# Output stores of 64 rows cut into two by rows, in a fused attention and GEGLU kernel

## The chip, the cores and the metric

The kernel runs on one core of a Trainium2 chip. A core has TensorE (matmul; PE in the profile, and PEld for its weight loads), VectorE (DVE), ScalarE (ACT), GpSimd (POOL) and SyncE (SP), each with its own stream of instructions that it works through in order, and 16 DMA engines that all of them share. The metric is the time of one launch on the device, in microseconds. Engines wait for each other, and for DMAs, on semaphores.

## The reference

Attention without softmax (scores are scaled, cut at zero, squared and divided by the length), then a GEGLU feed-forward block on the joined heads:

```python
scores = scale * np.matmul(q, k.transpose(0, 1, 3, 2))      # q, k, v: 8 x 12 x 448 x 64
attn = np.maximum(scores, 0.0) ** 2 / S
attn_out = np.matmul(attn, v)
x = attn_out.transpose(0, 2, 1, 3).reshape(B * S, H * D)    # 3584 x 768
g = x @ w_gate                                              # 768 x 1536
gelu = 0.5 * g * (1.0 + erf(g / sqrt(2)))
out = (gelu * (x @ w_val)) @ w_out                          # 3584 x 768, float32
```

## The kernel before

The eight batches go through four stages that overlap: loading q, k and v (GpSimd issues the loads, which turn float32 into bfloat16 on the way); transposing q and k per third of a batch's heads (by TensorE for the first two batches, afterwards by a regrouping copy on VectorE, `qkr`, L475, and two DMA transposes that SyncE issues, L480); scores, relu (ScalarE, L714), square (VectorE, L728) and the product with v; then the feed-forward block. TensorE works on quarters of its array (64 x 64), and matmuls for one half of the rows run beside those for the other. The products with the weights use seven multiplications for a 2 x 2 block of sub-matrices in place of eight, so sums and differences of operands are made on VectorE (`s`, `ts`, `ws`, `wt`).

The last product makes 28 tiles of 128 tokens by 768 columns. A tile consists of two chunks of 64 tokens, and lies in SBUF as `osb` (pool with four buffers). Its two column halves are opened by copies on ScalarE (L1225) and finished by additions on VectorE (L1223). A chunk's 64 rows lie in 64 partitions; in the output, row p of chunk c of a batch is row 7 p + c, so a store writes 64 rows of 3072 bytes that are 7 rows apart. `emit_store` (L1238) issues one chunk. Tiles are made in groups `gr` of two (t = 2 gr and 2 gr + 1), 14 groups in all. For the first twelve groups a tile's two chunks are stored whole by SyncE as soon as its two last additions are done (48 stores of 192 KB); for the last two groups (LAST = 2) the column halves are stored apart, chunk 0 by SyncE and chunk 1 by ScalarE (16 stores of 96 KB).

A planner (`run_plan`) places all instructions of all engines in an order once, when the program is built, from costs written in the code; the order then is fixed. An `osb` tile takes a buffer when its first copy is placed, and this copy waits in the program for all stores of the tile that had the buffer four tiles before. Scores go to one pair of PSUM banks (`sp`), so that the scores of the next unit wait for the relu of the last one.

SyncE's queue holds the DMA transposes and the stores in one order. A transpose may be held back until a given matmul has run, and waits for the transpose before it. All DMAs that SyncE and ScalarE issue take one of eight completion semaphores in turn, and an issue waits, where it isn't clear from the order anyway, for the DMA eight before it.

Of the kernel before, what the change touches and what calls it, by code (L numbers as in the profile page):

```python
# [276 lines left out]
def kernel(  # L277
# [10 lines left out]
    nc = tc.nc  # L288
# [6 lines left out]
    P = 64  # L295
# [5 lines left out]
    d_model, d_ff = moe_w_gate.shape  # L301
# [56 lines left out]
    HALF = (slice(0, P), slice(P, 2 * P))  # L358
# [744 lines left out]
                "7": lambda: wt_op[3, i]}[name]()  # L1103

    LAST, HELD = 2, 8
    sums, osb, stored = {}, {}, {}
    CUTS = 0, KH - 1, KH

# [51 lines left out]
    def add_product(at, gr, name, final):  # L1160
# [27 lines left out]
        else:  # L1188
            t, half = source
            have = [[st["made_by"](b, half * KH + f) for b in sorted({b for b, _ in chunks[t]})] for f in range(KH)]  # L1190

        def emit(r, fc):
# [4 lines left out]
            for j in range(2):  # L1197
# [13 lines left out]
                for fc in range(KH)] for r in range(2)]  # L1211
        st["last", name] = ops[1][-1]
        left, right = slice(0, OGS), slice(OGS, 2 * OGS)
        t, cols, added = {"1": (t0, left, False), "2": (t0, left, True), "3": (t0, right, False),
                          "6": (t1, left, False), "4": (t1, left, True),
                          "7": (t1, right, False), "5": (t1, right, True)}[name]
# [11 lines left out]
        engine = "DVE" if added else "ACT"  # L1228
# [9 lines left out]
        def emit_store(j, engine=nc.sync, part=slice(0, d_model)):  # L1238
            b, c = chunks[t % 2][j]
            rows = out[b * S:(b + 1) * S, :].rearrange("(p c) d -> c p d", c=SC)  # L1240
            return engine.dma_start(rows[c, :, part], osb[t][HALF[j], part])  # L1241

        def held_store(*args):
            def emit():
                ins = emit_store(*args)
                if op.mark is not None:
                    tc.add_manual_dep(ins.ins, op.mark.ins.name, SYNC, reason="pace")

            op = Op("SP", 0.6, emit, [rd] if len(args) > 1 else st["done", t], lag=0.0 if len(args) > 1 else 2.5, prio=-1)
            op.hold = gr >= HELD  # L1250
            return op

        if name in "2345":
            st["done", t] = [*st.get(("done", t), ()), rd]
            if gr >= B * SC // 4 - LAST:
                SP.append(held_store(0, nc.sync, cols))
                ACT.append(Op("ACT", 0.45, lambda: emit_store(1, nc.scalar, cols), [rd], prio=-1))
            elif len(st["done", t]) == 2:
                stored[t] = [held_store(j) for j in range(2)]
                SP.extend(stored[t])  # L1260
# [66 lines left out]
    for at, item in placed:  # L1327
# [4 lines left out]
        else:  # L1332
            _, gr, name = item
# [71 lines left out]
    for kind, lo, hi in pairs:  # L1405
        if kind == "with":
            upper.append((tau[place[lo]], hi))
        else:
# [8 lines left out]
            t = tau[min(behind + 1, len(PE0))]  # L1417
# [79 lines left out]
```

## Time and profile before

| what | value |
|---|---|
| time, median of 2 runs | 401.8 us (401.79 to 401.81) |
| span of the profiled execution, first to last instruction | 394.9 us |
| time less span: what lies around the program | 6.9 us (the profile gives no time of its own for its execution beside the span) |
| TensorE busy | 386.3 us, 98% |
| VectorE, ScalarE, GpSimd busy | 78%, 66%, 25% |
| DMA, mean | 114 GB/s, 85567 packets |
| mean granted TensorE clock | 0.998 |

In the lines below, an instruction's group is told as line, engine, operation and `out<-in` with the tile's names. "SPq" and "ACTq" are the sequencers of these engines, which wait and issue DMAs. In a timeline the columns are start, duration and what ran, with the idle time before it and what ended that in brackets. For a line or tile in a window, three numbers behind a count are the shortest, median and longest duration in ns, then the first and last start in us; "DMA to landing" is the time from a DMA's issue to its last completion. A row that begins with two times (a:b) is a stretch: its length, then for PE, PEld, DVE, ACT and POOL the busy time and the number of instructions, the granted TensorE clock, the DMA engines' mean busy share, and GB/s. A row of a DMA queue has packets, MB, and the time of its packets as a share of 16 engines' time in that stretch, which can go over 100% when packets overlap.

### The profile page before, as it was taken

How to read it: one execution, taken by the hardware profiler on the slowest of the kernel's cores; microseconds unless marked ns; L12 is line 12 of the kernel's file. 1: busy time of each engine (PE TensorE's matmuls, PEld its weight loads, DVE VectorE, ACT ScalarE, POOL GpSimd, SP SyncE). 2: the span in 40 equal slices, each digit the busy share in tenths (PEclk: the TensorE clock that was granted, in tenths of full speed). 3: DMA queues.
4: the chain of work that ended last, by engine and by line, in shares of the span. 5: the costliest groups of instructions: out<-in, count | busy, mean ns of one | idle time of the engine just before them, and what ended most of it. 6: DMA issues, size and time to landing. Idle time of an engine off the chain costs nothing.

```text
span 394.9 us, 22904 instructions
## 1 busy us (share of the span) xinstructions
PE 386.3 (98%) x10570; PEld 358.4 (91%) x10573; DVE 309.6 (78%) x522; ACT 258.7 (66%) x401; POOL 97.2 (25%) x156
## 2 busy tenths in 40 slices
PE   7999999999999999999999999999999999999995
PEld 3458889999999999999999999989999999999994
DVE  3885779968797499999797779758988999866772
ACT  5866872357677767787786478765787886535541
POOL 7656523322233323232332123310211000000000
PEclk9999999999999999999999999999999999999999
DMA  8999999988999969887999598880763501121134
GB/s 110 186 199 199 197 209 185 112 103 83 161 148 175 152 85 143 93 132 121 113 148 108 124 122 111 139 83 11 103 105 56 125 6 43 45 45 45 43 85 120
DMA packets 85567, 45.12 MB, mean 114 GB/s; under 512 B 46048, under 2 KB 82400, under 8 KB 85472
## 3 DMA queue, kind: packets, MB, share of 16 engines
q0 software_dynamic: 46944, 24.39, 49.9%
q1 hardware_dynamic: 37888, 18.49, 26.4%
q8 instruction: 82, 1.34, 1.4%
q10 hardware_dynamic: 640, 0.79, 0.6%
q14 instruction: 13, 0.11, 0.1%
HBM read 48.76 MB, written 11.01 MB: 151 GB/s over the span
## 4 chain that ended last, share of the span: by engine, by line
PE 93%; DVE 2%; DMA 2%; POOL 1%; issue 1%; ACT 0%; ACTq 0%; POOLq 0%
PE ff L365 85%; PE sp L365 7%; DMA qk<-in_k_dram 2%; DVE attnT L728 1%; PE sp L646 1%; POOL qk L424 1%; DVE xT L792 0%; PE ff L646 0%; ACTq L1241 0%; ACT osb L1225 0%; ACT rl L714 0%; PE ff L567 0%; DVE osb L1223 0%; DVE qkT L650 0%; POOL ident masks.py:199 0%
## 5 line engine op out<-in xcount | busy, mean ns | idle before, releaser
L714 ACT ACTIVATE rl<-sp 128x896 bf16<-128x896 f32 x168 | 152.1, 919 | 50.4 <-PE sp L365 45.1
L365 PE MATMUL ff<-xT,wg 64*64 64x224 bf16 (+1 forms) x2304 | 183.7, 299 | 0.6 <-issue 0.6
L365 PEld LDWEIGHTS <-wv 64*64 64x64 bf16 x2304 | 127.7, 107 | 4.4
L365 PEld LDWEIGHTS <-wg 64*64 64x64 bf16 x2304 | 123.3, 107 | 5.0 <-issue 0.5
L365 PE MATMUL ff<-xT,wv 64*64 64x448 bf16 x1056 | 120.8, 349 | 0.0
L728 DVE TENSOR_TENSOR attnT<-rl 128x1792 bf16<-128x1792 bf16 (+1 forms) x98 | 92.2, 952 | 6.6 <-ACT rl L714 6.2
L365 PEld LDWEIGHTS <-ws 64*64 64x64 bf16 x1872 | 92.3, 107 | 1.4 <-issue 1.0
L365 PEld LDWEIGHTS <-s 64*64 64x64 bf16 x1344 | 81.6, 107 | 1.8
L365 PE MATMUL ff<-attnT,v 64*64 64x448 bf16 (+1 forms) x768 | 79.7, 326 | 0.7 <-DVE attnT L728 0.6
L365 PE MATMUL ff<-ts,wv 64*64 64x224 bf16 x1248 | 78.7, 256 | 0.0
L365 PE MATMUL ff<-ts,ws 64*64 64x224 bf16 x1248 | 77.6, 256 | 0.0
L365 PE MATMUL sp<-qkT 64*64 64x448 bf16 (+1 forms) x768 | 74.6, 328 | 0.7 <-issue 0.3
L365 PE MATMUL ff<-wo,s 64*64 64x384 bf16 x672 | 63.4, 323 | 0.0
L966 DVE TENSOR_TENSOR part<-ff,part 128x448 f32<-128x448 f32 x78 | 47.5, 622 | 20.1 <-PE ff L365 16.4
L365 PEld LDWEIGHTS <-uT 64*64 64x64 bf16 x1008 | 62.5, 107 | 0.7
L365 PE MATMUL ff<-wt,s 64*64 64x384 bf16 x672 | 61.4, 322 | 0.0
L365 PE MATMUL ff<-wo,uT 64*64 64x384 bf16 x672 | 60.7, 322 | 0.0
L962 ACT COPY part<-ff 128x448 f32<-128x448 f32 x78 | 41.3, 534 | 12.4 <-PE ff L365 11.2
L443 POOL DMA_DIRECT2D v<-in_v_dram x48 | 29.6, 620 | 80.3 <-ACT rl L714 44.3
L365 PEld LDWEIGHTS <-v 64*64 64x64 bf16 x768 | 44.7, 107 | 4.1 <-issue 1.7
L424 POOL DMA_DIRECT2D qk<-in_q_dram x43 | 27.6, 642 | 80.0 <-ACT rl L714 59.5
L1049 DVE TENSOR_TENSOR uT<-gel,ff 128x448 bf16<-128x448 bf16 x44 | 27.3, 620 | 22.4 <-PE ff L365 11.0
(51 smaller groups left out, 423.9 us busy)
## 6 DMA issues: line engine op xcount, KB each, us to landing
out_dram<-osb SPq DMA_DIRECT2D x48, 192.0 KB, 3.3
v<-in_v_dram POOLq DMA_DIRECT2D x48, 128.0 KB, 4.1
wg<-in_moe_w_gate_dram POOLq DMA_DIRECT2D x6, 384.0 KB, 10.4
wv<-in_moe_w_val_dram POOLq DMA_DIRECT2D x6, 384.0 KB, 11.0
wo<-in_moe_w_out_dram POOLq DMA_DIRECT2D x4, 576.0 KB, 14.9
qk<-in_q_dram POOLq DMA_DIRECT2D x18, 128.0 KB, 3.5
qk<-in_k_dram POOLq DMA_DIRECT2D x18, 128.0 KB, 4.3
qk<-in_q_dram POOLq DMA_DIRECT2D x18, 96.0 KB, 3.8
```

Of the source, the lines that this page charges most:

```text
L365: ins = nc.tensor.matmul(o, lhsT, rhs, start=start, stop=stop, skip_group_check=onto, tile_position=(P * row, P * col))
L424: return nc.gpsimd.dma_start(qk16[b, m][HALF[i], r0:r0 + h1 - h0, cols], src[b, h0:h1].rearrange("h (p c) d -> p h (c d)", c=SC)[:, :, cols])
L443: return nc.gpsimd.dma_start(v16[b, m][HALF[i], h0 % 4:h0 % 4 + h1 - h0, :, :], v[b, h0:h1].rearrange("h (p c) d -> p h c d", c=SC)[:, :, ...
L646: blocks.add(nc.tensor.transpose(t[HALF[j], c, :], src[:, 2 * r + j, c, :], ident[:, :], tile_position=(0, P * j)))
L714: relu.ins = nc.scalar.activation(duo["rl"][:, u % 2, :, :], box[0][:, :, 0:S], AF.Relu).ins
L728: nc.vector.tensor_tensor(a[:, part], duo["rl"][:, part], duo["rl"][:, part], op=ALU.mult)
L962: rd.ins = nc.scalar.copy(st["t", name][:, :], box[0][:, 0:S]).ins
L966: rd.ins = nc.vector.tensor_tensor(t[:, :], box[0][:, 0:S], t[:, :], op=ALU.add).ins
L1049: u_op[b, fc].ins = nc.vector.tensor_tensor(uT[b][:, fc, :], gel.pop((b, fc))[:, :], box[0][:, 0:S], op=ALU.mult).ins
```

## The change

A store of all 768 columns from SyncE is cut by rows into two DMAs that are issued one behind the other, in the same place of the order. The place of the cut goes through a list of eight by the store's number (4 gr + 2 (t mod 2) + j): 64 (whole), 61+3, 57+7, 49+15, 55+9, 52+12, 56+8, 60+4. Each of the eight occurs six times among the 48 stores; 42 stores are cut. The half-width stores at the end are as before. What is stored, and from where, doesn't change. A wait on a particular matmul, where there is one, is attached to the first of the two.

```diff
     LAST, HELD = 2, 8
+    CUT = 64, 61, 57, 49, 55, 52, 56, 60
     sums, osb, stored = {}, {}, {}
...
         def emit_store(j, engine=nc.sync, part=slice(0, d_model)):
             b, c = chunks[t % 2][j]
             rows = out[b * S:(b + 1) * S, :].rearrange("(p c) d -> c p d", c=SC)
-            return engine.dma_start(rows[c, :, part], osb[t][HALF[j], part])
+            first = CUT[(4 * gr + 2 * (t % 2) + j) % len(CUT)] if engine is nc.sync and part == slice(0, d_model) else P
+            ins = engine.dma_start(rows[c, 0:first, part], osb[t][j * P:j * P + first, part])
+            if first < P:
+                engine.dma_start(rows[c, first:P, part], osb[t][j * P + first:(j + 1) * P, part])
+            return ins
```

The instructions of TensorE, VectorE, ScalarE and GpSimd are the same ones in the same order; SyncE's queue has 42 DMAs more, and the turn of the eight semaphores shifts accordingly. ScalarE's copy that takes over a buffer then waits for three or four DMAs of the former tile in place of two.

## The prediction

> **What bounds the kernel now.** I read the profiled execution's page first: span, busy shares, the chain that ended last, the DMA queues and the issues.
>
> ```profile
> span 394.9 us, 22904 instructions
> ...
> PE 386.3 (98%) x10570; PEld 358.4 (91%) x10573; DVE 309.6 (78%) x522; ACT 258.7 (66%) x401; POOL 97.2 (25%) x156
> ...
> q1 hardware_dynamic: 37888, 18.49, 26.4%
> ...
> PE 93%; DVE 2%; DMA 2%; POOL 1%; issue 1%; ACT 0%; ACTq 0%; POOLq 0%
> ...
> out_dram<-osb SPq DMA_DIRECT2D x48, 192.0 KB, 3.3
> ```
>
> TensorE is busy for 386.3 of 394.9 us and carries 93% of the last chain. So 394.9 - 386.3 = 8.6 us is all that any gain could come from, and whatever stops TensorE, which runs its instructions in a fixed order, is added whole. The 48 stores that change are not on the chain. The question is therefore what a later landing of a store holds up. Three things can wait for one: the next DMAs on the same queue, above all the transposes that feed the scores; the reuse of one of the four osb buffers, which ScalarE opens with a copy; and the end of the program. For that I went through SyncE's timeline and the copies, looking for the store whose landing has the least time behind it. It is the first one that is cut in the changed kernel, the second half of the first osb tile. SyncE around it:
>
> ```profile
> 101.39 2.08 SPq L480 DMA_TRANSPOSE qkT<-qkr  x1
> 103.53 1.22 SPq L1241 DMA_DIRECT2D out_dram<-osb  x2
> 105.96 1.25 SPq L480 DMA_TRANSPOSE qkT<-qkr  x1
> 107.26 1.22 SPq L1241 DMA_DIRECT2D out_dram<-osb  x2
> 109.21 1.26 SPq L480 DMA_TRANSPOSE qkT<-qkr  x1
> ```
>
> The pair at 103.53 is the whole store (64 rows) and the one that becomes 61+3; the pair at 107.26 becomes 57+7 and 49+15. The first pair by source line and window (the second is issued at 104.2), then ScalarE's copies into osb in a window of their own, then ScalarE's and TensorE's timelines:
>
> ```profile
> L1241 SPq DMA_DIRECT2D out_dram<-osb x2: 582/588/593, 103.5 to 104.2; - x2
> ...
> DMA to landing us min/median/max: 3.9/4.9/5.8
> ```
> ```profile
> L1225 ACTq EVENT_SEMAPHORE  x1: 1275/1275/1275, 108.8 to 108.8; - x1
> ```
> ```profile
> 110.07 0.48 ACT L1225 COPY osb<-ff 128x384 f32<-128x384 f32 x1 [0.41 <-PE ff L365]
> 110.44 0.92 ACT L714 ACTIVATE rl<-sp 128x896 bf16<-128x896 f32 x1
> ...
> 115.11 0.48 ACT L1225 COPY osb<-ff 128x384 f32<-128x384 f32 x1 [0.55 <-PE ff L365]
> ```
> ```profile
> 111.51 0.44 PE L365 MATMUL sp<-qkT 64*64 64x224 bf16 x8
> ```
>
> The second store lands at 104.2 + 5.8 = 110.0. ScalarE's sequencer stands in a wait from 108.8 for 1.275 us, until 110.0, and its copy starts at 110.07. This copy is the fifth tile's first write and in the program waits for every store of the first tile, since it takes over its buffer. The idle time is put down to a matmul, but the landing is equally late: no cover is left. Behind the copy on ScalarE stands a relu (110.44 to 111.36), which frees the one pair of PSUM banks into which the scores at 111.51 go. TensorE has 0.15 us to spare.
>
> **The change part by part.** Six stores stay whole; the 42 others become two, so SyncE issues 42 more DMAs. Its issue takes 0.59 us (row above): 25 us on an engine that mostly waits, at most 1.2 us a pair of stores. I cost that at nothing; without the cover it would be part of the landing times below. Every engine's own order is as before, and the semaphores only rotate.
>
> What matters is how the rows are dealt out. A window with two whole stores and little else, as DMA queues:
>
> ```profile
> DMA packets 161, 0.41 MB, mean 137 GB/s; under 512 B 32, under 2 KB 32, under 8 KB 160
> ...
> q1 hardware_dynamic: 160, 0.39, 60.3%
> ```
>
> 160 packets are 128 rows and 32 small ones: 64 rows and 16 small packets a store, one small packet for each DMA engine and four rows each. All DMAs on this queue have row counts that 16 divides, so how 61 rows go isn't shown. The ends: dealt as evenly as can be (at most four rows an engine, no cost), or only in equal shares, and then 61, a prime, goes to one engine, 57 to three by 19, 49 to seven by 7, and 55, 52, 56 and 60 to 11, 13, 14 and 15 by five or four. Equal shares are what the rows show wherever I look, so I take the second end.
>
> The Trainium skill, "DMA: Bandwidth & Descriptors", section "Why a DMA increments its semaphore by 16 and not by 1", says that a DMA of this kind uses the largest count up to 16 that divides the slowest dimension, and that 127 partitions go to one engine. By it the sum would be the one below; no run here shows it yet.
>
> Price of a row on one engine, from two windows that hold stores (0.97 us and 2.10 us long):
>
> ```profile
> q1 hardware_dynamic: 220, 0.40, 108.5%
> ```
> ```profile
> q1 hardware_dynamic: 152, 0.39, 86.0%
> ```
>
> 0.40 MB are 130 rows of 3072 bytes in 0.97 us on 16 engines: 0.12 us a row, for stores that had queued behind a transpose (110.08 to 111.05). 0.39 MB in 2.10 us give 0.26 us, for stores that met empty queues and may have been limited by their issue (329.8 to 331.9). 57 rows of a 61-row store queue behind others of their own, which is like the first: 0.12.
>
> The sum:
> 1. The busiest engine gets 61 rows where it had four: 57 x 0.12 = 6.8 us later, landing at 116.8. The ends: 5.5 (the engine that gets them may have been done 1.3 us before the last one, since the landing of 110.0 is that of the slowest) and 57 x 0.26 = 14.8. Loads that share this engine are in between: two are issued on GpSimd at 108.3 and 110.0, some 2 us of it at most, and the next wait for a stalled ScalarE.
>
> ```profile
> 108.31 0.99 POOL L424 DMA_DIRECT2D qk<-in_q_dram  x1 [3.84 <-ACT rl L714]
> 109.96 0.61 POOL L424 DMA_DIRECT2D qk<-in_q_dram  x1 [0.66 <-ACT rl L714]
> ```
>
> 2. ScalarE's copy, relu and TensorE's scores all move by 6.8 us: +6.8. DVE, and the transposes that come next, gain that time, so they don't add.
> 3. The copy of 115.11 needs the stores of 107.26: 19+1+7+1 = 28 rows behind the 61 on one engine, 3.4 us and a transpose of about 1 us, against 5.04 us between the two copies. Nothing, with an end of 3.
> 4. TensorE stands still for more than 6 us, and its clock falls when it does. Stretches at the end, and the warm-up at the start beside the scores:
>
> ```profile
> 390.00:390.80 0.80, 0.73 (x10) 0.30 (x5) 0.00 (x0) 0.27 (x1) 0.00 (x0) 1.00 0.79 221
> 390.80:393.00 2.20, 0.00 (x0) 0.00 (x0) 0.00 (x0) 0.48 (x1) 0.00 (x0) 1.00 0.72 191
> 393.00:394.90 1.90, 0.00 (x0) 0.00 (x0) 0.00 (x0) 0.00 (x0) 0.00 (x0) 0.55 0.13 45
> ```
> ```profile
> L365 PE MATMUL sp<-qkT 64*64 64x448 bf16 (+1 forms) x768 | 74.6, 328 | 0.7 <-issue 0.3 <-ACT qkT L617 0.2
> L1430 PE MATMUL ff<-warm 128*64 128x512 bf16 x16 | 3.3, 590 | 1.2 <-DVE table L353 1.2
> ```
>
> TensorE ends at 390.7, and the mean of 0.55 from 393.0 on is that of a clock which goes to a half at about 393.2, some 2.4 us later. The first matmuls, 590 ns for 512 columns against 328 for 448, show the slow state, for the 3.3 us that they last. Half speed for 3.3 us loses 1.7. Ends: 0 (no fall) and 3.3.
>
> The Trainium skill, "TensorE: Matmul & The Clock Gate", section "Part 1: The HAM clock gate (the "warmup" mystery)", puts the fall after an idle window of about 3.4 us and the return after a busy one. By that the term would be the same 1.7; the trace's 2.4 us is shorter, and the trace holds no stall within the work.
>
> 5. The five other stores of 61 rows (issued at 146.0, 222.0, 249.4, 310.3, 355.0). The tightest follow-ups:
>
> ```profile
> L480 SPq DMA_TRANSPOSE qkT<-qkr x1: 1222/1222/1222, 152.4 to 152.4; - x1
> DMA to landing us min/median/max: 4.6/4.6/4.6
> ```
> ```profile
> 170.24 0.35 PE L365 MATMUL sp<-qkT 64*64 64x448 bf16 x1
> ```
> ```profile
> L1225 ACT COPY osb<-ff x6: 479/480/482, 377.9 to 384.8; 128x384 f32<-128x384 f32 x6
> ```
>
> The transpose behind the store of 146.0 lands at 157.0, and the scores that read it (the fourteenth of 24 thirds, 32 matmuls each of the x768) begin at 170.24: 13.2 us of cover for 6.8. The last 61-row store, at 355.0, is wanted by the second of the copies from 377.9 on. Nothing; with rows at 0.26 us the first would be late by 1.6.
>
> Sum: 6.8 + 0 + 1.7 + 0 = 8.5. The profiled execution's span is 394.9, and the median of the runs lies 6.9 above it, which stays: 401.8 + 8.5 = 410.3, rounded to 410.5 (+2.2%). What a measurement of this kernel can tell from no change is 2%, or 8.0 us: up to 409.8.
>
> **The rivals.**
> - Short stall: 5.5 us, and the clock stays or the phase is kind: 407 to 409. For it: the landing's 5.8 us belongs to the slowest engine. Against: the loads in between.
> - Costlier rows: 0.26 us a row, or ScalarE waiting a second time (step 3) and one transpose late: 14.8 + 1.7 + 3 + 1.6 = 21, so up to 422; a part of it gives 413 to 418.
> - Not slower: the change doesn't do what I say, since 61 rows are dealt four to an engine. The landing stays near 110.0, only the 0.6 us for issuing three more rows may show: 401.8 to 402.4. It decides in favour of this as soon as the first cut store lands within 6 us of its issue. For it: every DMA in the trace uses all 16 engines.
> - Faster by 2% would need nearly all of the 8.6 us in which TensorE is idle, most of which no store touches.
>
> **How the numbers follow.** Forecast 0.48 (own range 408.5 to 413), short stall 0.22, costlier 0.17, even dealing 0.12, faster 0.01. The range 404 to 418 leaves out even dealing (0.12), faster (0.01) and the top of the costlier case (0.06). Slower: 0.17 and 0.41 of the forecast's 0.48, whose lower edge is within 2%: 0.58. Same: 0.22 + 0.12 + 0.07 = 0.41. Faster: 0.01.
>
> **What would show it.** Right: SyncE's first cut store takes 12 us or so to land, while the later ones of 55, 52, 56 and 60 rows stay at about 4; ScalarE idles once for some 7 us before a copy into osb near 110, released by the DMA of osb; TensorE has one hole of that length there; the granted clock dips in the stretch after it; no hole near 170. Wrong: a first cut store that lands after 4 to 6 us refutes the dealing; a long landing without a hole refutes the link over ScalarE; a hole elsewhere, before scores, would mean that the transposes are late after all.

## The result and the profile after

The changed kernel took **440.2 us** (median of two runs, 438.2 and 442.2) against 401.8: a ratio of 1.096, interval 1.084 to 1.107. The forecast was 410.5 and its range ended at 418. The direction was right, the size was wrong by 30 us. The execution that was profiled is the one of 442.2 us. In what follows a time is the median of all runs and a loss the difference of two such medians, while the ratios leave out the slow runs (over 1.5% above the fastest of their kernel); without these the loss of the two moved stores would be 3.7 us in place of 4.2, and no other would change by more than 0.2 us.

The page of the changed kernel's profile: span, busy times, the granted clock in 40 slices, the queue that carries the stores, and the engines' shares of the chain that ended last.

```profile
span 440.3 us, 22984 instructions
...
PE 397.9 (90%) x10570; PEld 362.1 (82%) x10573; DVE 309.9 (70%) x522; ACT 259.1 (59%) x401; POOL 96.7 (22%) x156
...
PEclk9999999999889996899999998986999999999998
...
q1 hardware_dynamic: 37948, 18.49, 33.6%
...
PE 84%; issue 6%; DMA 3%; DVE 3%; SPq 1%; POOL 1%; ACT 1%; ACTq 0%; POOLq 0%
```

The same bytes go through the queue (18.49 MB), 42 of the 80 instructions more are the stores' DMAs, and the other engines run the same number of operations. Yet TensorE now stands still for 42 us in place of 8.6, and "issue" has come into the chain with 6%. Which instruction stood, and behind what, is told by the waits of TensorE (what waited, what it waited for, total us, times, longest), first before, then after:

```profile
PE ff L365 <- issue: 0.6, 1, 0.6
PE ff L646 <- DMA qk<-in_k_dram: 0.6, 1, 0.6
```
```profile
PE ff L365 <- issue: 25.6, 8, 8.6
PE sp L365 <- ACT rl L714: 6.5, 2, 6.4
PE ff L646 <- DMA qk<-in_k_dram: 2.5, 2, 2.1
```

These three rows and TensorE's busy time account for the span's growth of 45.4 us: issue 25.6 - 0.6 = 25.0, relu 6.5, start-up 2.5 - 0.6 = 1.9, busy 397.9 - 386.3 = 11.6, together 45.0. The second row is the hole of the forecast. The first one isn't in the forecast at all.

**The forecast's hole.** ScalarE's timeline of the changed kernel around it (start, duration, what ran, in brackets the idle time before it and what ended it):

```profile
110.13 0.86 ACT L1226 COPY osb<-ff 128x384 f32<-128x384 f32 x2
110.98 0.92 ACT L714 ACTIVATE rl<-sp 128x896 bf16<-128x896 f32 x1
118.99 0.48 ACT L1226 COPY osb<-ff 128x384 f32<-128x384 f32 x1 [7.09 <-DMA out_dram<-osb]
119.36 0.92 ACT L714 ACTIVATE rl<-sp 128x896 bf16<-128x896 f32 x1
```

The copy waited for the store, the relu behind it freed the PSUM banks, and the scores came 6.4 us late. That is the forecast's chain (steps 1 and 2) with 6.4 in place of 6.8 us.

**The other holes.** Three more are long, and end at 172.32, 267.15 and 299.09 (8.62, 3.88 and 8.65 us). SyncE's and then TensorE's timeline around the first of these:

```profile
158.64 0.97 SPq L1243 DMA_DIRECT2D out_dram<-osb  x2
159.66 0.60 SPq L1245 DMA_DIRECT2D out_dram<-osb  x1
160.36 17.02 SPq L480 DMA_TRANSPOSE qkT<-qkr  x2
```
```profile
163.10 0.60 PE L365 MATMUL ff<-xT,wg 64*64 64x448 bf16 x12
172.32 0.58 PE L365 MATMUL ff<-xT,wv 64*64 64x448 bf16 x2 [8.62 <-issue]
```

L1243 at 158.64 is a whole store and the 61 rows, L1245 the 3 rows, and behind them SyncE issues a DMA transpose at 160.36 (the other one of this row follows at 176.2, after the hole). Three microseconds later TensorE stops, within the feed-forward block, whose operands are made on VectorE and have nothing to do with a store. The profile finds nothing that it waits for. What the DMA engines did in that time (packets, mean rate; per queue packets, MB, share of 16 engines; then the issues, with the time to landing), first the changed kernel, then the kernel before in the same stretch, 163.9 to 171.5:

```profile
DMA packets 92, 0.17 MB, mean 22 GB/s; under 512 B 27, under 2 KB 43, under 8 KB 92
...
q1 hardware_dynamic: 52, 0.15, 5.3%
q0 software_dynamic: 40, 0.02, 1.7%
...
qk<-in_k_dram POOLq DMA_DIRECT2D x1, 96.0 KB, 11.6
```
```profile
DMA packets 2106, 0.76 MB, mean 101 GB/s; under 512 B 1352, under 2 KB 2104, under 8 KB 2104
...
q0 software_dynamic: 1070, 0.48, 53.7%
q1 hardware_dynamic: 1034, 0.25, 20.9%
q8 instruction: 2, 0.03, 1.8%
```

In the changed kernel 92 packets pass where there were 2106. A share of 5.3% + 1.7% is about one of 16 engines (6.25%): that of the engine with the 61 rows. The others aren't idle, they are held. These are the queues of the stretch just ahead, 163.0 to 163.95, again the changed kernel first:

```profile
q1 hardware_dynamic: 176, 0.07, 849.2%
q0 software_dynamic: 96, 0.04, 513.6%
```
```profile
q1 hardware_dynamic: 315, 0.08, 96.4%
q0 software_dynamic: 12, 0.01, 5.6%
```

The time of a packet counts where it begins, so packets that begin there stay open for long. In the packet records, 15 of them have 256 bytes, a size that on this queue only the transposes have (32256 packets, 896 for each of 36), and 9 belong to loads. All 24 end between 171.7 and 171.9. In the kernel before no packet is open for more than 2.1 us. A load that is issued in this stretch takes 11.6 us to land. And the instruction queue q8, with two packets before, has none. I call this stretch a jam. It ends at about 171.8 us, and then everything passes at once: 517 packets, all under 512 B, from 171.8 to 173.0.

A second queue of kind "instruction", q14, has a packet in the jam too. It began at 162.2, so it stands in the window 160.0 to 163.5 of the changed kernel:

```profile
q14 instruction: 1, 0.01, 17.2%
```

17.2% of 16 engines' 3.5 us are 9.6 us for one packet; in the kernel before these packets take 0.3 to 1.0. It lands at 171.8, and TensorE resumes at 172.3. All this points to **TensorE having run out of instructions**, and a count bears it out. Number TensorE's records (matmuls, weight loads and waits, 21177 in this trace) in their order. This hole begins behind number 6590, and the other stops "behind issue" of over 1 us behind 5566, 9662, 11454 and 12734: each time 190 more than a multiple of 256. The same holds for all 35 stops behind "issue" of 0.25 us and more that the twelve traces have after the first 30 us (193 more in the two traces that hold three more matmul records). The forecast's hole lies elsewhere, behind number 4524, 172 more than a multiple of 256. One packet of q8 comes for every 258 records (82 packets). So TensorE stops where a portion of its instructions ends, whatever it computes there.

### The profile page after: what moved, and what is told of

It reads as the page before. It is cut to its first block, busy times and chain, and to the rows that moved or that the text cites. A ratio compares the mean times of both kernels' runs of the same rounds, so it can differ in the third digit from the quotient of the medians.

```text
span 440.3 us, 22984 instructions
## 1 busy us (share of the span) xinstructions
PE 397.9 (90%) x10570; PEld 362.1 (82%) x10573; DVE 309.9 (70%) x522; ACT 259.1 (59%) x401; POOL 96.7 (22%) x156
## 3 DMA queue, kind: packets, MB, share of 16 engines
q1 hardware_dynamic: 37948, 18.49, 33.6%
q8 instruction: 82, 1.34, 1.3%
## 4 chain that ended last, share of the span: by engine, by line
PE 84%; issue 6%; DMA 3%; DVE 3%; SPq 1%; POOL 1%; ACT 1%; ACTq 0%; POOLq 0%
PE ff L365 76%; PE sp L365 7%; DMA qk<-in_k_dram 2%; DVE attnT L728 2%; DMA out_dram<-osb 2%; SPq L1243 1%; DVE xT L792 1%; PE sp L646 1%; POOL qk L424 1%; SPq L1245 1%; ACT rl L714 0%; PE ff L646 0%; ACT osb L1226 0%; DVE uT L975 0%; ACTq L1243 0%
## 5 line engine op out<-in xcount | busy, mean ns | idle before, releaser
L365 PE MATMUL ff<-xT,wg 64*64 64x224 bf16 (+1 forms) x2304 | 188.1, 303 | 8.6 <-issue 8.6
L365 PEld LDWEIGHTS <-wv 64*64 64x64 bf16 x2304 | 130.0, 108 | 22.0 <-issue 17.6
L365 PEld LDWEIGHTS <-wg 64*64 64x64 bf16 x2304 | 125.0, 108 | 14.7 <-issue 10.3
L365 PE MATMUL ff<-xT,wv 64*64 64x448 bf16 x1056 | 125.5, 359 | 10.4 <-issue 10.4
L365 PEld LDWEIGHTS <-ws 64*64 64x64 bf16 x1872 | 93.9, 109 | 3.2 <-issue 2.7
L365 PE MATMUL ff<-ts,wv 64*64 64x224 bf16 x1248 | 80.9, 258 | 5.0 <-issue 4.9
L365 PE MATMUL sp<-qkT 64*64 64x448 bf16 (+1 forms) x768 | 76.0, 335 | 7.1 <-ACT rl L714 6.5
L365 PE MATMUL ff<-wt,s 64*64 64x384 bf16 x672 | 62.9, 329 | 0.0
L365 PE MATMUL ff<-wo,uT 64*64 64x384 bf16 x672 | 61.9, 326 | 0.0
L365 PEld LDWEIGHTS <-qkT 64*64 64x64 bf16 x768 | 36.9, 108 | 12.5 <-issue 10.0
## 6 DMA issues: line engine op xcount, KB each, us to landing
wo<-in_moe_w_out_dram POOLq DMA_DIRECT2D x4, 576.0 KB, 15.7
```

The source lines that it names most:

```text
L365: ins = nc.tensor.matmul(o, lhsT, rhs, start=start, stop=stop, skip_group_check=onto, tile_position=(P * row, P * col))
```

## The experiments

The theory after the result, JAM: a DMA transpose that SyncE issues behind a 61-row store is opened on all DMA engines, but on the one engine with the rows it has to queue behind them. Until it gets there, the other 15 engines serve nobody else; loads and TensorE's instructions wait. The rivals: many cut stores together do it (each a little); or the rows wait on ScalarE or on late transposes, as in the forecast. Each ratio below is against runs of the kernel before on the same chip. Their median was between 398.8 and 399.4 us there, so each loss is given within its own batch.

**Which cuts cost.** First the 61+3 stores alone, everything else but these cut, and a cut in two shares that 16 divides. The first edit is this one; in the other two the list is `64, 64, 57, 49, 55, 52, 56, 60`, and `64, 48, 48, 48, 48, 48, 48, 48`.

```diff
-    CUT = 64, 61, 57, 49, 55, 52, 56, 60
+    CUT = 64, 61, 64, 64, 64, 64, 64, 64
```

> Only the six stores with the first cut (61+3) are cut; the other 42 are whole. Theory JAM: a DMA transpose that stands behind the 61 rows in the queue is open on 15 DMA engines until the one with the rows gets to its share; until then these engines serve nobody, TensorE's instruction fetch included. It expects most of the loss of the changed kernel, since its four long holes (6.4, 8.6, 3.9, 8.6 us) each follow a 61-row store with a transpose behind it: 428 to 440 us. Rival SCALARE (the prediction as recorded: only the reuse of the first osb buffer): one hole, 410.5 us. Rival COUNT (42 more DMAs and the shifted turn of the semaphores): 6 of 42 additional DMAs, so about 407 us.

> The 61+3 cuts are left whole; the other six cuts stay (36 more DMAs). JAM: the longest share of one engine is 19 rows (57+7), 15 more than before at 0.13 us, so jams of some 2 us more, mostly hidden: 402 to 410 us. SCALARE: nothing of the first hole is left, 402 us. COUNT: 36 of 42 DMAs are still there, 430 us or more.

> The same 42 stores are cut, but into 48+16 rows, both of which go to all 16 engines in equal shares. JAM and SCALARE: no engine has more rows than before, 401.5 to 403 us. COUNT: 435 us or more.

| kernel | us | before in its batch | loss | ratio (interval) | TensorE busy | longest holes, us |
|---|---|---|---|---|---|---|
| 61+3 alone (six stores cut) | 434.0 | 398.8 | +35.2 | 1.087 (1.080 to 1.093) | 395.0 | 6.4, 8.3, 3.1, 8.6 |
| all but 61+3 (36 stores cut) | 404.2 | 398.8 | +5.3 | 1.013 (1.007 to 1.018) | 387.9 | 2.6, 1.2, 1.1, 1.0 |
| 48+16 (42 stores cut) | 400.0 | 398.8 | +1.2 | 1.004 (1.001 to 1.008) | 388.4 | 0.7 |

Six stores make 35.2 us, against 38.4 for all the cuts together. The number of DMAs costs next to nothing: 42 more of them, in shares that 16 divides, cost 1.2 us. So what decides is how many rows one engine gets. The Trainium skill, "DMA: Bandwidth & Descriptors", section "Why a DMA increments its semaphore by 16 and not by 1", says that a DMA of this kind takes the largest number of engines up to 16 that divides the rows; these runs agree, since 61, which only 1 divides, is the dear one.

**One place or another.** Then the first 61-row store alone (number 1), two of the later ones (numbers 9 and 25, in front of the jams near 165 and 290 us), and two very late ones (33 and 41, behind which SyncE issues no transpose).

```diff
-    CUT = 64, 61, 57, 49, 55, 52, 56, 60
+    ONLY = 1,
...
-            first = CUT[(4 * gr + 2 * (t % 2) + j) % len(CUT)] if engine is nc.sync and part == slice(0, d_model) else P
+            first = (61 if 4 * gr + 2 * (t % 2) + j in ONLY else 64) if engine is nc.sync and part == slice(0, d_model) else P
```

In the other two it is `ONLY = 9, 25` and `ONLY = 33, 41`.

> Only the first 61+3 store of the program is cut, the one on which the prediction rested. SCALARE as recorded: landing 6.8 us later, one hole of that length near 112 us, slow clock after it, 410.5 us (408.5 to 413). JAM expects the same hole, since the copy into osb and the jam of the transpose behind it end together: 408 to 412 us. If the hole comes without the slow clock, 408.5.

> Only the second and the fourth 61-row store (numbers 9 and 25) are cut, in their place, each directly ahead of a DMA transpose. In the changed kernel each was followed by a hole of 8.6 us in TensorE without a wait for data. JAM: two holes of 8 to 9 us and about 2 us each of slow clock after them: 17 to 23 us above the kernel before. SCALARE (reuse of osb as the only link): these buffers are wanted some 35 us later, so no more than 1 us above it.

> Only the last two 61-row stores (numbers 33 and 41) are cut; all transposes are issued by then. JAM: nothing open on the other engines, 0 to 1 us above the kernel before, and the DMA engines' mean busy share stays low while the rows run. HOG: two holes as long as the others, 10 to 20 us above.

The first store alone: 407.0 us, +8.2, ratio 1.018 (1.012 to 1.025). The sum of the forecast was 8.5. TensorE's waits show the one hole, 6.6 us, behind the relu, and stretches of this run (us, then PE, PEld, DVE, ACT, POOL busy with counts, granted clock, DMA share, GB/s) what the clock does after it:

```profile
PE sp L365 <- ACT rl L714: 6.6, 1, 6.6
```
```profile
114.00:118.00 4.00, 0.07 (x4) 0.07 (x7) 0.00 (x0) 1.42 (x3) 0.00 (x0) 0.50 0.64 81
118.00:122.00 4.00, 4.00 (x56) 2.94 (x59) 1.09 (x1) 1.88 (x4) 1.22 (x2) 0.50 1.11 225
122.00:126.00 4.00, 4.00 (x84) 3.14 (x79) 1.90 (x4) 2.38 (x4) 0.67 (x2) 0.77 0.31 36
126.00:130.00 4.00, 4.00 (x112) 3.67 (x108) 2.97 (x5) 2.65 (x5) 1.16 (x2) 1.00 0.95 144
```

The clock is at a half before the hole ends (117.9) and is back only in the third stretch, some 6 us after work resumed. TensorE is busy for 390.0 us, 3.7 more than before. The slow clock makes 3.0 of these, half of the 5.9 us that TensorE worked at it (117.9 to 123.8). Where the clock never fell within the work, TensorE is busy for 387.1 to 388.4 us, so 0.8 to 2.1 us come without it.

The two later stores: 421.0 us, **+21.9**, ratio 1.057 (1.048 to 1.066), though the forecast had them at nothing. Their holes are 8.0 and 8.5 us, and TensorE is busy for 393.9, 7.6 more. After the holes it worked for 6.0 and 4.7 us at half the clock, which makes 5.3 of the 7.6. The same picture in the DMA engines, in the jam (267.0 to 274.0) and in the stretch behind it (274.7 to 278.6):

```profile
DMA packets 77, 0.16 MB, mean 22 GB/s; under 512 B 1, under 2 KB 31, under 8 KB 77
...
q1 hardware_dynamic: 46, 0.14, 5.3%
q0 software_dynamic: 31, 0.02, 1.6%
```
```profile
DMA packets 1540, 0.56 MB, mean 143 GB/s; under 512 B 1042, under 2 KB 1538, under 8 KB 1538
...
q8 instruction: 1, 0.02, 1.9%
```

TensorE resumes at 278.6, after that one instruction packet (276.1 to 277.3 in the trace's records). And the two very late stores cost nothing: 400.0 us against 399.1 in their batch, ratio 1.000 (0.996 to 1.004), no hole over 0.6 us behind the start-up. Their rows run at the same time as matmuls that lack nothing, here the queue from 316.0 to 320.0 and TensorE in a stretch around it:

```profile
DMA packets 39, 0.12 MB, mean 30 GB/s; under 512 B 4, under 2 KB 4, under 8 KB 38
...
q1 hardware_dynamic: 38, 0.10, 6.5%
q8 instruction: 1, 0.02, 2.0%
```
```profile
313.00:321.00 8.00, 8.00 (x271) 7.92 (x266) 7.64 (x14) 7.25 (x13) 0.00 (x0) 1.00 0.30 75
```

One engine alone carries 0.10 MB in 4 us, 25 GB/s or 0.12 us a row, as in the jam. But an instruction packet passes meanwhile and TensorE is busy for all of the 8 us. So a slow store by itself isn't enough; something behind it is needed. By this time the loads are over too (no row of q0), so this run alone doesn't tell transposes from loads.

**The same two stores, behind the transposes.** The test that JAM asks for: the same rows on the same single engine, issued after the next two (or three) transposes in SyncE's queue.

```diff
+    put_off = []
...
             one[:] = [ins]
+            for late in [*put_off]:
+                late[0] -= 1
+                if not late[0]:
+                    late[1]()
+                    put_off.remove(late)
...
+            def cut(tile=osb[t]):
+                ins = engine.dma_start(rows[c, 0:first, part], tile[j * P:j * P + first, part])
+                if first < P:
+                    engine.dma_start(rows[c, first:P, part], tile[j * P + first:(j + 1) * P, part])
+                return ins
             if first < P:
+                put_off.append([{9: 2, 25: 3}[4 * gr + 2 * (t % 2) + j], cut])
+                return None
+            return cut()
```

> The same two stores with the same cut, but issued later in SyncE's queue: number 9 behind the next two transposes, number 25 behind the next three, where the following transpose is some 8 and 14 us away. Same bytes, same engine, same number of DMAs; all other orders as before. JAM: the rows are nearly or wholly done when the next transpose comes, so 0 to 5 us above the kernel before. Rival HOG (the engine that carries the rows is the one that TensorE's instructions come through, or 8 us of rows starve something else, transposes or not): as the kernel with the stores in place, 17 to 23 us above.

SyncE's timeline around the first of the two:

```profile
152.52 1.57 SPq L481 DMA_TRANSPOSE qkT<-qkr  x1
154.15 0.46 SPq L1250 DMA_DIRECT2D out_dram<-osb  x1
154.67 0.30 SPq L1252 DMA_DIRECT2D out_dram<-osb  x1
160.84 1.38 SPq L481 DMA_TRANSPOSE qkT<-qkr  x1
```

The 61 rows (issued at 154.15) are alone with the loads until SyncE issues the next transpose, 6.7 us later. The time was 403.3 us: +4.2 in place of +21.9, ratio 1.008 (1.004 to 1.012), and the longest hole 1.6 us in place of 8.5. This is the experiment that carries the explanation: the bytes, the rows and the engine count are the same, and only the place before or behind the transposes differs. It also shows both cases within one trace. Beside the rows passed, from 156.0 to 162.0 and then, with the next transpose open, from 163.8 to 165.9:

```profile
q0 software_dynamic: 762, 0.34, 52.4%
q1 hardware_dynamic: 40, 0.12, 6.0%
q8 instruction: 1, 0.02, 1.0%
```
```profile
q0 software_dynamic: 14, 0.01, 2.2%
```

Beside the rows alone 762 load packets and one of instructions pass in 6 us; with a transpose behind the rows, 14 and none in 2.1 us. In the packet records the rows last from 155.9 to 166.1, 10.2 us and not 61 x 0.12 = 7.3, as load packets take turns with them. The transpose meets their end, which fits the rest of 4.2 us: stops behind "issue" of 1.6, 1.6, 0.7 and 0.7 us follow.

**Half the length, and another queue.** A 62-row share goes to two engines, 31 rows each (`CUT = 64, 62, 64, 64, 64, 64, 64, 64`, six stores). And the two stores of 61 rows, in their old place but issued by ScalarE, so that the transposes don't stand behind them in the same queue and the engine can take turns:

```diff
-            ins = engine.dma_start(rows[c, 0:first, part], osb[t][j * P:j * P + first, part])
+            ins = (engine if first == P else nc.scalar).dma_start(rows[c, 0:first, part], osb[t][j * P:j * P + first, part])
```

> The six stores of the first cut become 62+2 in place of 61+3; the others are whole. If equal shares decide, 62 rows go to two engines, 31 each, 3.9 us behind each other in place of 8. JAM: jams of about 4 us in place of 8, of which some 3 us are covered by instructions already there: holes of 0.5 to 2 us and hardly any slow clock, 4 to 14 us above the kernel before. A cost in proportion to the rows on an engine would be 35 x 31 / 61 = 18 us. If it is the odd row count as such, as with 61: 35 us.

> As the kernel with the second and fourth 61-row store cut in place, but ScalarE issues the 61 rows (SyncE the other 3), on a queue of its own; the following transpose is no longer behind the rows in one queue. JAM by order in the queue alone: the transpose passes, 0 to 4 us above the kernel before. JAM also by turns on the engine: its 48 to 64 packets there take turns with rows of 0.13 us each, 6 to 8 us, so the jam is nearly as long: 12 to 20 us above.

The 62-row stores cost 23.0 us (422.1, ratio 1.059, 1.053 to 1.066), with holes of 3.1, 5.7, 1.2 and 5.4 us. I had expected 4 to 14, reckoning that TensorE has some 3 us of instructions in hand that shorten the hole. It has them, and they shorten nothing: the two long holes behind "issue" begin 4.3 and 5.6 us after their jams do (at 273.1 after 268.8, at 160.9 after 155.3) and end 4.4 and 5.7 us after the jams are over (278.5 after 274.1, 166.6 after 160.9). Fetching and starting again takes as long as the stock lasts, so a hole is as long as its jam, 5.4 and 5.7 us here. The cost falls with the length of the rows, but less than in proportion: 23.0 us against 35.2, some two thirds for half the rows.

ScalarE's queue helped only a little: 416.1 us, +16.7 in place of +21.9, ratio 1.045 (1.038 to 1.051), holes of 7.9, 6.6 and 1.3 us. This is within the 12 to 20 us for turns on the engine. The transposes behind the two stores land 14.6 and 15.7 us after their issue, in place of 17.5 and 16.2, as if they took turns with the rows on their engine and finished nearly as late as behind them. The Trainium skill, "DMA: Bandwidth & Descriptors", section "Queues, rings and completion order", has each DMA engine take its queues in turn, packet by packet; this run fits it for the one engine. What that rule doesn't lead one to expect is how little the 15 others pass meanwhile: from 152.0 to 159.0 it is 155 load packets and none of the instruction queue.

**The first store, behind the transposes.** The same move for number 1 alone (`{1: 2}`). If only ScalarE's wait counts there, the loss must stay.

> Only the first 61+3 store is cut, and is issued behind the next two transposes, so that no transpose is open behind it until TensorE goes on. What is left is the prediction's link alone: ScalarE's copy into the fifth osb tile waits for the landing. SCALARE: rows from about 111, landing near 119.5, a hole of 8 to 9.5 us before scores, released by ScalarE, and 3.7 us of slow clock as in the kernel with the store in place: 9 to 13 us above the kernel before. If the hole of the kernel with the store in place came from the jam and not from the copy: 0 to 2 us.

407.9 us, +8.5, ratio 1.024 (1.019 to 1.029): it stays, with 8.2 for the store in its place. ScalarE's timeline:

```profile
115.44 0.48 ACT L1232 COPY osb<-ff 128x384 f32<-128x384 f32 x1
116.12 0.92 ACT L720 ACTIVATE rl<-sp 128x896 bf16<-128x896 f32 x1 [0.20 <-PE sp L365]
123.48 0.48 ACT L1232 COPY osb<-ff 128x384 f32<-128x384 f32 x1 [6.44 <-DMA out_dram<-osb]
```

A copy waits for the store again, though a later one than before (123.48 in place of 116.58): with the later issue the buffers change hands in another order. TensorE has holes of 1.4 and 5.0 us in place of 6.6. This is less clean than it looks: a transpose issued at 119.08 also meets the end of the rows, and a jam of 2.7 us (120.7 to 123.4) lies within the second hole. The loss is a little under the 9 to 13 us that were expected, and so is the hole. Neither hole lies at a place where a portion of instructions ends. The run agrees with the forecast's chain; it doesn't rule out that the jam, by holding up the landing, has a part in those 5.0 us.

## Why the prediction was wrong, point by point

- **The dealing of the rows** (61 to one engine) and **the price of a row** (0.12 us) were right: the single engine moves 25 GB/s while it moves rows. But other packets take turns there, so the 61 rows lasted 10 to 11 us in these records, and not 7.3. That 42 more DMAs cost nothing was right too (48+16: +1.2 us).
- **Steps 1 and 2**, the store that lands late and the way over ScalarE's copy and relu to the scores, were right: 6.4 us of hole in the changed kernel and 6.6 with this store alone, against 6.8. The whole sum of 8.5 us is what this one store costs (8.2). That the landing came out so near was in part luck. With this store alone the 61 rows ran from about 105.4 to 116.0, longer than in the sum. But they also began earlier than the sum has it: it counts from the landing of 110.0, and in the kernel before the last row of this pair was moved by 108.3.
- **Step 3**, no second wait for the copy that follows, was right: there is no second hole there.
- **Step 4**, the slow clock, was right, and for the forecast's own hole in size too. In the changed kernel this hole ends at 120.34, and the clock is back at 123.7:

```profile
120.34:123.70 3.36, 3.36 (x48) 2.54 (x51) 1.09 (x1) 1.76 (x3) 1.22 (x2) 0.50 1.38 159
123.70:127.00 3.30, 3.30 (x88) 2.79 (x81) 1.58 (x3) 1.79 (x3) 0.61 (x1) 1.00 1.37 85
```

  Half of 3.36 us are the 1.7 of the forecast. Over all holes that lowered the clock, TensorE worked for 2.6 to 6.0 us at half speed, which loses 1.3 to 3.0 us each; the forecast's ends were 0 and 3.3. The Trainium skill, "TensorE: Matmul & The Clock Gate", section "Part 1: The HAM clock gate (the "warmup" mystery)", has windows of some 3.4 us that run freely. The slow stretches in these records are 3.4, 6.8 and 10.2 us long, multiples of it, so the trace agrees. That the size was met so well is in part luck: with the same store alone the slow clock cost 3.0 us.
- **Step 5 is the one that failed**: "The five other stores of 61 rows", summed as "Nothing". I asked who waits for the data of those stores, and for the data of the transposes behind them, and found 13.2 us of cover. That cover was real: the scores came to wait for no transpose. I did not ask what the DMA engines do for others while a transpose hangs behind the rows. That costs three long holes and two short ones in the changed kernel, 8.62 + 3.88 + 8.65 + 1.35 + 1.77 = 24.3 us (the last one behind a 57+7 store), and the slow clock behind the long ones, 14.8 us of work at half speed, so 7.4 us more. Together that is some 32 us. The miss is 30 us by the medians, and 37 by the two spans, which grew by 45.4; there the start-up has 1.9, and 2.5 us of TensorE's busy time are left that no slow clock explains.
- **What was in the trace of before** and could have said so: the instruction queue's packets stand on its page, and in its records five packets of a transpose behind a pair of stores are open from 107.8 to 109.9. The chain of waits has no line for this, since TensorE's instructions came in time but for one stop of 0.6 us.
- **The signs** named beforehand did their work. A hole "elsewhere" was named as a refutation, though with the wrong reason behind it ("the transposes are late after all"): the holes lie before feed-forward matmuls, and their releaser is "issue".
- **The 6.9 us around the span** are no property of the program. In the runs of before beside the experiments, time and span lie 2.0 to 3.7 us apart; the rest was the distance between the profiled execution of before and the two timed runs. As the sum was put on the median as a difference, this moved nothing much, but it wasn't something "which stays". In its own execution the changed kernel lies 1.9 us above its span.

How the instruction packets and the holes lie in time: the packet records of the changed kernel and of the runs with 61+3 alone, two stores, and 62+2 have ten holes of 3 us and more behind "issue" after a jam. In nine of them the instruction queue q8 passes no packet during the jam, its next one starts 1.4 to 2.3 us after the jam's end, and TensorE resumes 1.3 to 1.6 us after that packet has landed; the short hole ending at 144.97 too comes 1.4 us after a packet, and so does the one of 0.6 us in the kernel before (1.5). In the tenth, the one that ends at 172.32, no q8 packet lies between, only the one of q14 that was open for 9.6 us. It lies at one of the counted places as well, but the last q8 packet had landed at 162.56, so what held TensorE there until 172.32 stays open. No run moved these packets alone. Nor was it tried whether another DMA in the transpose's place would hold the engines too: all those behind the rows here that jammed were transposes, and the very late stores, with only plain stores behind them, jammed nothing.

## What to carry to other kernels

Cut a DMA where 16 divides both parts (48+16: +1.2 us), and never put a DMA that lands on one or two engines ahead of a DMA transpose: two such stores cost 21.9 us there, 4.2 behind the transposes, and nothing where no transpose followed; another issuing queue hardly helps. When TensorE is idle behind "issue", look at the DMA queues in that window, the instruction queue above all: the question to ask of a slow transfer is not only who waits for its data, but who shares the engines with what is queued behind it.

## What the runs showed of the hardware

- A DMA transpose behind rows on one engine of 16 holds the others too: 24 packets of transpose and loads stayed open for 7.8 to 8.9 us, and 92 packets passed in 7.6 us, 22 GB/s, where the kernel before moved 2106 at 101 GB/s.
- The packets of the instruction queue (82, 1.34 MB, some 16 KB each) don't pass in such a jam either, and TensorE stops 190 records above a multiple of 256. In the nine regular holes TensorE goes on for 4 to 7 us into a jam and needs 4 to 6 us to get going after it, so jams of some 5 us cost 3 to 6 us each already.
- All holes of 3.1 to 8.7 us within the work put the clock to a half, and it stayed there for 2.6 to 6.0 us after work resumed, which cost another 1.3 to 3.0 us a hole. Holes up to 2.6 us didn't lower it (mean clock 0.999 in the run without 61-row stores).
